# Turning the second batch's first half by DMA instead of on TensorE, in a fused attention and SwiGLU kernel

## The chip, the cores and the metric

One core of a Trainium2 chip. The metric is the device time of the whole kernel in microseconds (us), median of several runs. "Slot" below is a place in the kernel's own schedule, not a time: two slots per step of the feed-forward part. PE is TensorE, ACT ScalarE, DVE VectorE, POOL GpSimd, SP SyncE. A transfer lands when all its completions are counted. A packet is one DMA record of the trace: 1024 or 512 bytes of a load, 256 of a transpose.

## The reference, cut to what matters

```python
def _attn_ref(q, k, v, E, F):                 # q, k, v: (8, 8, 1024, 64), E, F: (64, 1024)
    k_proj = einsum('ks,bhsd->bhkd', E, k)
    v_proj = einsum('ks,bhsd->bhkd', F, v)
    scores = q @ k_proj^T / sqrt(64)
    attn   = softmax(scores)                  # 64 columns
    return attn @ v_proj
x   = attn_out as (8192, 512)                 # tokens x (heads * 64)
g   = x @ w_gate;  val = x @ w_val            # 512 x 1536
out = (g * sigmoid(g) * val) @ w_out          # 1536 x 512
```

## The kernel before

Each of the 8 batches is cut into two halves of 512 tokens. While PE does the feed-forward part of one half, the attention units of a later one are strewn between its matmuls. Two turns are needed in each half: q (so that heads' channels lie on the partitions) and the softmaxed attention (so that its 64 columns do). They are done on PE or by a DMA transpose:

```python
BY_DMA = [(b, ch) for b in range(1, B) for ch in range(CH)][1:]   # all but batch 0 and half (1, 0)

def u_T(b, u):                # q turn on PE: four transposes, one copy
    for n in range(4):
        nc.tensor.transpose(out=ps[:, n, :], in_=..., identity=ident_bf[:])
    copy(eng, t[:], ps[:])

def u_TD(b, ch):              # q turn of a half by DMA, on SP's queue
    nc.sync.dma_start_transpose(out=t[:], in_=qb[b, ch][:]...)

def u_AD(b, ch):              # attention turn of a half by DMA, on SP's queue
    nc.sync.dma_start_transpose(out=t[:]..., in_=AA.pop((b, ch, "d"))[:]...)

def u_S(b, u): ...            # scores on PE, exp on ACT
def u_R(b, u): ...            # sum and reciprocal on DVE
def u_N(b, u): ...            # normalise on POOL, into AA (PE turn) or AAd (DMA turn)
def u_PV(b, ch, pr): ...      # PE: attention times v, reads AT
```

The loads `load_q`, `load_k`, `load_v` and those of weights are issued by POOL and cast from f32 to bf16 on the way, so the place of a load among POOL's `u_N` units decides when it starts. [...] The q, k and v pools hold enough buffers for the next batch.

The softmax here doesn't subtract the row's maximum and nothing guards it: scores larger than these inputs give would overflow.

## Time and profile before

| | before |
|---|---|
| median | 573.17 us (572.98 to 573.52, 4 runs) |
| PE busy | 564.2 of 571.7 us |
| PE's waits after 33 us | none over 0.2 us |
| DMA engines, 0 to 86 us | full |
| DMA transposes | 26, landing 4.3 to 17.5 us after issue |

How to read it: PE sets the time, so only PE work or a wait of PE counts. The first 86 us, in which the DMA engines are full, are where a transfer can come too late. The lines are in the prediction.

### The profile page before, as it was taken

The numbers are of one execution on the slowest core, as the hardware profiler recorded it, in microseconds if no ns is written. First come the engines' busy times: TensorE is split into PE (matmuls) and PEld (weight loads), VectorE is DVE, ScalarE is ACT, GpSimd is POOL, SyncE is SP. The second block draws the span as 40 slices with busy tenths as digits, with TensorE's granted clock in tenths as the row PEclk, the third lists the DMA queues.
The fourth block names the chain that finished last, engine by engine and source line by source line (L and its number), as shares of the span: only waits on it lengthen the run. The fifth ranks groups of instructions, "written<-read, shape, count | busy, mean of one in ns | idle before, by whom it ended". The sixth has DMA issues, their size and how long they took to land.

```text
span 571.7 us, 7944 instructions
## 1 busy us (share of the span) xinstructions
PE 564.2 (99%) x2971; PEld 268.5 (47%) x2971; DVE 336.6 (59%) x581; ACT 238.3 (42%) x421; POOL 109.2 (19%) x122
## 2 busy tenths in 40 slices
PE   8999999999999999999999999999999999999997
PEld 4644444444444444444444444444444444444444
DVE  3677566666466654666556665567546674554540
ACT  3555434354435434444335434354342543443232
POOL 6834121134002500124001330023200220000000
PEclk9999999999999999999999999999999999999999
DMA  9999993549901697038940499204990124100012
GB/s 202 176 199 206 202 177 77 89 71 197 202 29 47 113 192 148 19 75 129 196 100 37 64 176 196 63 20 90 196 176 37 44 50 75 38 37 23 33 38 92
DMA packets 106983, 61.86 MB, mean 108 GB/s; under 512 B 60096, under 2 KB 98240, under 8 KB 106944
## 3 DMA queue, kind: packets, MB, share of 16 engines
q0 software_dynamic: 42800, 29.36, 35.7%
q1 hardware_dynamic: 63232, 30.42, 24.7%
q10 hardware_dynamic: 912, 1.57, 1.0%
q8 instruction: 23, 0.38, 0.3%
q14 instruction: 16, 0.13, 0.1%
HBM read 60.29 MB, written 16.78 MB: 135 GB/s over the span
## 4 chain that ended last, share of the span: by engine, by line
PE 92%; DMA 3%; DVE 2%; POOL 1%; ACT 1%; issue 0%; DVEq 0%; POOLq 0%
PE yps L362 29%; PE vps L324 27%; PE gps L324 27%; PE kvp L149 3%; PE sc L229 2%; PE pv L287 2%; DMA wv<-in_moe_w_val_dram 2%; DMA qb<-in_q_dram 1%; DVE zz L244 1%; POOL AA L260 0%; POOL wg L117 0%; PE qTp L195 0%; DVE hT L348 0%; ACT xT L137 0%; DVE s L343 0%
## 5 line engine op out<-in xcount | busy, mean ns | idle before, releaser
L343 DVE SCALAR_TENSOR_TENSOR s<-th,gps 128x512 f32<-128x512 f32 x192 | 130.5, 680 | 139.2 <-ACT th L336 138.8
L324 PE MATMUL gps<-xT,wg 128*128 128x512 bf16 (+1 forms) x776 | 197.8, 377 | 0.7 <-DMA wg<-in_moe_w_gate_dram 0.4
L324 PE MATMUL vps<-xT,wv 128*128 128x512 bf16 (+1 forms) x776 | 197.5, 377 | 0.1
L362 PE MATMUL yps<-wo,hT 128*128 128x512 bf16 (+1 forms) x780 | 194.5, 376 | 0.0
L336 ACT ACTIVATE th<-gps 128x512 f32<-128x512 f32 x192 | 114.6, 597 | 163.4 <-PE gps L324 161.9
L348 DVE TENSOR_TENSOR hT<-s,vps 128x512 bf16<-128x512 f32 x192 | 132.0, 687 | 22.1 <-PE vps L324 1.5
L362 PEld LDWEIGHTS <-hT 128*128 128x128 bf16 x780 | 76.2, 98 | 89.9
L260 POOL TENSOR_TENSOR AAd<-ee,rr 128x512 bf16<-128x512 f32 x52 | 54.1, 1040 | 319.5 <-issue 178.1
L324 PEld LDWEIGHTS <-wv 128*128 128x128 bf16 x776 | 73.8, 98 | 83.2 <-issue 3.3
L324 PEld LDWEIGHTS <-wg 128*128 128x128 bf16 x776 | 74.0, 98 | 81.9 <-DMA wg<-in_moe_w_gate_dram 0.9
L372 ACT ACTIVATE ysb<-yps 128x512 f32<-128x512 f32 (+1 forms) x65 | 38.4, 590 | 78.1 <-PE yps L362 78.1
L137 ACT CAST xT<-pv 128x512 bf16<-128x512 f32 x63 | 36.7, 584 | 51.2 <-PE pv L287 50.3
L244 DVE TENSOR_REDUCE zz<-ee 128x8 f32<-128x512 f32 x64 | 43.5, 679 | 19.4 <-ACT ee L233 19.4
L233 ACT ACTIVATE ee<-sc 128x512 f32<-128x512 f32 x64 | 37.9, 596 | 18.0 <-PE sc L229 17.9
L287 PE MATMUL pv<-AT,BDV 128*128 128x512 bf16 x60 | 22.6, 379 | 0.0
L229 PEld LDWEIGHTS <-qTd 128*128 128x128 bf16 x208 | 16.0, 98 | 12.3
L229 PE MATMUL sc<-BD,qTd 128*128 128x128 bf16 x208 | 20.1, 219 | 0.0
L137 DVE CAST BDV<-kvp 64x256 bf16<-64x256 f32 x14 | 6.0, 427 | 22.1 <-ACT ks L159 19.1
L260 POOL TENSOR_TENSOR AA<-ee,rr 128x512 bf16<-128x512 f32 x11 | 11.4, 1038 | 36.3 <-DVE rr L246 34.4
L246 DVE RECIPROCAL rr<-zz 128x8 f32<-128x8 f32 x64 | 13.0, 203 | 6.7 <-DVE zz L244 0.5
L149 PE MATMUL kvp<-vb,FT 128*64 128x512 bf16 (+2 forms) x80 | 15.7, 339 | 0.3 <-ACT BDV L137 0.3
L149 PE MATMUL kvp<-kb,ET 128*64 128x512 bf16 (+1 forms) x72 | 15.5, 358 | 0.3 <-DVE kb L137 0.2
(51 smaller groups left out, 146.4 us busy)
## 6 DMA issues: line engine op xcount, KB each, us to landing
out_dram<-ysb SPq DMA_DIRECT2D x63, 256.0 KB, 2.4
qb<-in_q_dram POOLq DMA_DIRECT2D x15, 512.0 KB, 16.9
kb<-in_k_dram POOLq DMA_DIRECT2D x7, 1024.0 KB, 11.3
vb<-in_v_dram POOLq DMA_DIRECT2D x7, 1024.0 KB, 14.0
wo<-in_moe_w_out_dram POOLq DMA_DIRECT2D x2, 768.0 KB, 15.3
wg<-in_moe_w_gate_dram POOLq DMA_DIRECT2D x5, 256.0 KB, 9.6
wv<-in_moe_w_val_dram POOLq DMA_DIRECT2D x5, 256.0 KB, 10.2
kraw<-in_k_dram ACTq DMA_DIRECT2D x2, 512.0 KB, 5.0
```

The costliest lines, as they stand in the source:

```text
L137: (nc.scalar.copy if eng is nc.scalar else eng.tensor_copy)(out=out, in_=in_)
L149: nc.tensor.matmul(out=t[lo : lo + 64, h0:h1].rearrange("p h d -> p (h d)"), lhsT=w[:, j, :], rhs=src[b][:, h0:h1, j, :], start=(j == 0), ...
L229: nc.tensor.matmul(out=ps[:, n, :], lhsT=t[:, n, :], rhs=BD[b % 2][:, 4 * g + n, :], start=True, stop=True)
L233: nc.scalar.activation(out=e[:].rearrange("p h j k -> p (h j k)"), in_=ps[:].rearrange("p a k -> p (a k)"), func=AF.Exp, scale=scale,)
L244: nc.vector.reduce_sum(out=z[:], in_=e[:], axis=AX.X)
L260: eng.tensor_tensor(out=a.rearrange("p j h k -> p h j k"), in0=ee.pop((b, u))[:], in1=rr.pop((b, u))[:].unsqueeze(3).to_broadcast([P, 4, 2 ...
L324: nc.tensor.matmul(out=ps[:, ts], lhsT=(wg, wv)[w][:, kt, f * P : (f + 1) * P], rhs=x[:, kt, ts], start=(kt == 0), stop=(kt == NKT - 1),)
L336: nc.scalar.activation(out=th[:], in_=ps[:], func=AF.Tanh, scale=0.5)
L343: nc.vector.scalar_tensor_tensor(out=s1[:], in0=th[:], scalar=1.0, in1=g[:], op0=ALU.add, op1=ALU.mult)
L348: nc.vector.tensor_tensor(out=hT[c][:, f, :], in0=s1[:], in1=ps[:], op=ALU.mult)
L362: nc.tensor.matmul(out=yy[c][:, cs], lhsT=hT[c][:, f, i * P : (i + 1) * P], rhs=wo[:, f, cs], start=(f == 0), stop=(f == NFT - 1),)
L372: nc.scalar.activation(out=ysb[:, cs], in_=yy[c][:, cs], func=AF.Copy, scale=0.5)
```

## The change

Its intent: take the last 32 turns of the second batch off PE. To make room for the two added DMA transposes, the first q half and k of the second batch are loaded ahead of the output weights, the projections and scores are moved, and the third batch's loads, whose k and v were issued at 47.6 and 48.5 us until now, wait on POOL behind the fourth normalised unit, that is until the input of the attention transpose is ready.

```diff
-BY_DMA = [(b, ch) for b in range(1, B) for ch in range(CH)][1:]
+BY_DMA = [(b, ch) for b in range(1, B) for ch in range(CH)]
 ...
         if b == 1:
+            put(22, u_TD, 1, 0)
+            put(29, u_KV, 1, "k")
+            put(32, u_KT, 1)
+            put(40, u_KV, 1, "v")
+            sa = (35, 36, 37, 38, 43, 44, 45, 47)
+            put(41, u_AD, 1, 0)
             put(30, u_TD, 1, 1)
-            put(34, u_KV, 1, "k")
-            put(36, u_KT, 1)
-            put(40, u_KV, 1, "v")
-            sa = (37, 38, 39, 40, 48, 50, 52, 54)
-            tt = (35, 36, 37, 38)
-            ta = (41, 42, 43, 44)
-            put(57, u_AD, 1, 1)
-            sp = (43, 44, 45, 46, 66, 67, 68, 69)
+            put(50, u_AD, 1, 1)
+            sp = (44, 45, 46, 46, 66, 67, 68, 69)
         else:
-            put(s0, u_KV, b)
+            put(s0 + (6 if b == 2 else 0), u_KV, b)
 ...                                       # the third batch's other units move a few slots too
+        load_q(1, 0)
+        load_k(1)
         load_wo(0)
         load_wo(1)
-        load_k(1)
 ...
-            s0 = 48 * (b - 1) - (12 if b == 2 else 24)
-            put(s0, load_k, b)             # and v, q, q two slots apart
+            s0 = 48 * (b - 1) - (20 if b == 3 else 24)
+            at = (40, 40, 41, 42) if b == 2 else (s0, s0 + 2, s0 + 4, s0 + 6)
+            put(at[0], load_k, b)          # and v, q, q at at[1], at[2], at[3]
```

More of the change, by code (lines that the diff above doesn't have):

```diff
@@ L394, in place @@
         if b == 1:
-            put(30, u_TD, 1, 1)
-            put(34, u_KV, 1, "k")
-            put(36, u_KT, 1)
-            put(40, u_KV, 1, "v")
-            sa = (37, 38, 39, 40, 48, 50, 52, 54)
-            tt = (35, 36, 37, 38)
-            ta = (41, 42, 43, 44)
-            put(57, u_AD, 1, 1)
-            sp = (43, 44, 45, 46, 66, 67, 68, 69)
-        else:
-            put(s0, u_KV, b)
-            put(s0 + 3, u_KT, b)
-            o = 14 if b == 2 else 6
-            put(s0 + (3 if b == 2 else -6), u_TD, b, 0)
-            put(s0 + (5 if b == 2 else -4), u_TD, b, 1)
+            put(22, u_TD, 1, 0)
[4 more added lines that the diff above has]
+            put(41, u_AD, 1, 0)
+            put(30, u_TD, 1, 1)
+            put(50, u_AD, 1, 1)
+            sp = (44, 45, 46, 46, 66, 67, 68, 69)
+        else:
+            put(s0 + (6 if b == 2 else 0), u_KV, b)
+            put(s0 + (9 if b == 2 else 3), u_KT, b)
+            o = 13 if b == 2 else 6
+            put(s0 + (7 if b == 2 else -6), u_TD, b, 0)
+            put(s0 + (9 if b == 2 else -4), u_TD, b, 1)
             sa = [s0 + o + 3 * j for j in range(NJ)]
@@ L414, in place @@
         for j in range(NJ):
-            if (b, j // 4) not in BY_DMA:
-                put(tt[j], u_T, b, j)
-                put(ta[j], u_A, b, j)
             put(sa[j], u_S, b, j)
@@ L549 @@
         put(23, u_PV, 0, 1, 3)
-        put(20, load_q, 1, 0)
         put(20, load_v, 1)
@@ L555 @@
         for b in range(2, B):
-            s0 = 48 * (b - 1) - (12 if b == 2 else 24)
-            put(s0, load_k, b)
-            put(s0 + 2, load_v, b)
-            put(s0 + 4, load_q, b, 0)
-            put(s0 + 6, load_q, b, 1)
+            s0 = 48 * (b - 1) - (20 if b == 3 else 24)
+            at = (40, 40, 41, 42) if b == 2 else (s0, s0 + 2, s0 + 4, s0 + 6)
+            put(at[0], load_k, b)
+            put(at[1], load_v, b)
+            put(at[2], load_q, b, 0)
+            put(at[3], load_q, b, 1)
         for s in slots:
```

## The prediction

> **What bounds the kernel now.** I read the page's busy shares and slices first, then PE's own waits, then PE's instructions in order of time, then the DMA transposes. The page:
>
> ```profile
> PE 564.2 (99%) x2971; PEld 268.5 (47%) x2971; DVE 336.6 (59%) x581; ACT 238.3 (42%) x421; POOL 109.2 (19%) x122
> ...
> PE   8999999999999999999999999999999999999997
> ...
> DMA  9999993549901697038940499204990124100012
> ```
>
> Each digit is one fortieth of 571.7 us, 14.3 us. PE is full in every slice but the ends; no other engine passes 59%. The DMA engines are full in the first six slices, 0 to 86 us, which is where all of the second batch's preparation lies. So the change can gain only PE time, and can lose only where a late transfer makes PE wait.
>
> PE's waits, in us, times, longest:
>
> ```profile
> PE efp L455 <- DMA Eraw<-in_E_dram: 0.8, 1, 0.8
> PE gps L324 <- DMA wg<-in_moe_w_gate_dram: 0.4, 1, 0.4
> PE kvp L149 <- ACT BDV L137: 0.3, 1, 0.3
> ```
>
> These and the other six all fall before 33 us. In the windows from 58 us to 560 us PE is busy for the whole of every window: no idle time can absorb or hide anything there.
>
> PE in order of time (start, duration, line) around the turns that the change removes:
>
> ```profile
> 62.47 0.39 PE L195 MATMUL qTp<-ident_bf,qb 128*128 128x128 bf16 x4
> 62.69 1.03 PE L324 MATMUL gps<-xT,wg 128*128 128x512 bf16 x4
> ...
> 75.17 0.39 PE L276 MATMUL aTp<-ident_bf,AA 128*128 128x128 bf16 x4
> 75.39 1.03 PE L324 MATMUL gps<-xT,wg 128*128 128x512 bf16 x4
> ```
>
> What counts is start to next start: four turns hold PE 62.47 to 62.69, 0.22 us, 55 ns each, though their records say 0.39 us together and 219 ns each. The ends are modelled and overlap.
>
> The transposes by DMA, as they are already done for the other 13 half batches (issue time in ns min/median/max; then us from issue to landing):
>
> ```profile
> L207 SPq DMA_TRANSPOSE qTd<-qb x13: 1782/3082/7293, 63.0 to 423.2; - x13
> ...
> DMA to landing us min/median/max: 4.3/4.9/13.0
> ```
> ```profile
> L214 SPq DMA_TRANSPOSE AT<-AAd x13: 1316/3715/8099, 102.6 to 472.1; - x13
> ...
> DMA to landing us min/median/max: 4.3/5.7/17.5
> ```
>
> The spread is the point: 4.3 us on idle DMA engines (the one issued at 102.6), 13.0 (issued at 63.0) and 17.5 (issued at 125.7) when loads run beside it.
>
> **What the Trainium skill says.** "TensorE: Matmul & The Clock Gate", Back-to-back issue gap, gives N/2.4 + 2.5 ns for one warm matmul, 56 ns at 128 columns and 216 at 512, but 81 and 131 for a sustained stream. This trace agrees with the first pair (55 ns a turn; four 512-column matmuls every 0.86 us, 216 each) and not with the second. Part 4 of that page, PE-mode transpose, has about 275 ns in one kernel's context; here a record is 219 ns and the spacing 55, and the spacing is the cost. "DMA: Bandwidth & Descriptors", Queues, rings and completion order, says that a DMA engine serves its queue rows in turn, packet by packet. The packet records agree: between 67.5 and 72.5 us each half microsecond has 74 to 77 load packets of 1024 bytes and 74 to 78 transpose packets of 256 bytes, where the transpose alone gets about 425 and the load alone about 102. A transpose has 2048 data packets, so beside such loads it needs about 13.4 us, alone 2.4.
>
> **The change, part by part.** Only the first half of the second batch still turned on PE.
>
> Removed from PE: four q turns and four attention turns of four instructions, 32 x 55 ns = 1.76 us. The eight spacings read directly (0.22, 0.24, 0.22, 0.22 and 0.22, 0.23, 0.22, 0.22) sum to 1.79. All of it is in saturated PE time, so all of it is on the path that sets the end. The built order confirms it: 64 PE rows less (32 loads of weights, 32 matmuls), and nothing added on PE.
>
> Removed beside PE: four ACT copies of 0.58 us and four DVE copies of 0.4 us. Worth nothing, neither bounds.
>
> Added: two DMA transposes on SP's queue and their wait for data. PE pays only if one is late. I place them from landings in the trace of before: the last value weights land at 38.6 to 40.1 us; a q half takes 2.65 us of full DMA, a k or v 5.05, half of wo 3.8.
>
> (a) First q half and k are now issued ahead of wo. Estimates: q lands at 42.5, k at 47.6. The k projection now stands at about 52.7 us on PE (two and a half f steps earlier than its 58.0): 5 us to spare.
>
> (b) The q transpose goes out at 42.5. The one at 63.0 showed its first packet 3.5 us after issue; then 13.4 us beside loads of wo and v: it lands at about 60. Its first user, the scores, stands at about 62.7 on PE. To spare: 2 to 3 us. wo then lands at 52.6 and 57.7, needed at 58.4 and 61.0: enough.
>
> (c) The second q half lands at about 66 instead of 63.0. Its transpose then meets idle engines, since the third batch's loads are held back, and lands near 70.8. PE uses it at about 77.
>
> (d) The attention transpose is the tight one. The fourth scores stand at 66.8 on PE; exp, the sum behind a 0.69 us hT on DVE, and 1.04 us on POOL end at about 70.9. SP issues then, and POOL lets k and v of the third batch go at the same moment. The first product with v stands at about 78.8: 7.9 us. Alone it takes 4.3; beside full loads from the first packet it would take 14. But a load that starts on idle engines starts slowly: after the one issued at 121.6 there were 33 packets in the microsecond from 123.0 to 124.0, and at full rate about 204. So the transpose should have most of its packets through before the loads fill: estimate 5.5 to 7.5 us, so landing between 76.4 and 78.4.
>
> (e) The third batch's k and v, issued at 47.6 and 48.5 before, now go at about 71; v lands near 87 to 89. The change moves its projection six slots later, to about 94.
>
> Later batches keep their work; their loads shift by four slots at most. Sum with no new wait: 573.08 - 1.76 = 571.3 us.
>
> **The rivals.**
>
> 1. A late attention transpose takes the place of the removed work. For it: round robin with 1024-byte packets, the 13.0 and 17.5 us seen, and a release of loads at the very same instant. Against it: the slow start of those loads, and the extra slots between the fourth unit and the first product. If the loads win from the first packet, it lands at about 85 and PE waits 6 us: 577.5, slower by 0.8%. A mild case is 1 to 2 us of wait: 572.5 to 573.5, no gain at all.
>
> 2. A late q transpose, case (b). For it: it runs wholly beside loads, and 17.5 us was seen. Against it: the 17.5 had an output queued ahead of it, this one has nothing. At 17.5 it would land at 60.0, still before 62.7. Its cost, if any, is 1 to 2 us.
>
> 3. The third batch's v or q too late for the moved projection, since the loads start 22 us later. For it: they carry about 15 us of DMA work, and two transposes and outputs share it. Against: the slack of 5 us or more. Beyond it PE would stall at about 94 us.
>
> 4. DMA becomes the bound everywhere. Against it: after 86 us the slices hold zeros and fours, and the bytes added are two transposes beside 26.
>
> **Range and chances.** No gain above about 1.8 us exists to be had, so the low end is 571.3 less the noise of some 0.3 and a little for a neighbouring gap: 570.8. I give 0.3 to a wait in rival 1, mean 2 us, and about 0.1 each to 2 and 3, of 1 to 2 us; high end 574.3. The middle: 571.5. Two per cent is 11.5 us. Nothing can win that, and only several late transfers together could lose it.
>
> **What would show it.** Right: 64 rows less on PE; busy PE down from 564.2 to about 562.4; no PE wait after 33 us; the attention transpose of this half in 5 to 8 us. The step that fails is visible by name: a PE wait of pv on AT is rival 1, of sc on qTd rival 2, of kvp on vb or kb at about 94 us rival 3. My placing of the loads is wrong if the q transpose lands after 61 us or the third batch's v after 92. The prediction is wrong beyond its range if PE idles over 3 us between 50 and 130 us, or if time goes that I have no part for.

## More of the kernel before

The granted clock is the share of its full clock that the profile shows TensorE to have had.

## The result, and the profile after

579.80 us median (579.32 to 580.27, 4 runs) against 573.17: slower by 6.6 us. The ratio is 1.0115, 95% interval 1.0097 to 1.0132. A ratio here is the mean time of one kernel's fast runs over that of the other's of the same rounds, so it is not quite the ratio of the medians quoted.

The page of the changed kernel, busy shares and slices:

```profile
PE 561.2 (97%) x2883; PEld 267.3 (46%) x2939; DVE 335.2 (58%) x577; ACT 236.7 (41%) x417; POOL 109.1 (19%) x122
...
PE   8999959999999999999999999999999999999997
...
PEclk9999989999999999999999999999999999999999
DMA  9999899508950499027970299413991023010002
```

PEld has 32 instructions less (2971 to 2939), as the built order said. Some matmul records are missing, so the loads of weights are the better count. New is the 5 in PE's sixth slice, 72 to 87 us, and the 8 in the clock beside it: PE stood still there, once. The list of PE's waits names it:

```profile
PE pv L287 <- DMA AT<-AAd: 5.9, 1, 5.9
```

And PE in order of time (start, duration, line, and in brackets the idle time before):

```profile
78.22 0.39 PE L229 MATMUL sc<-BD,qTd 128*128 128x128 bf16 x4
84.50 0.61 PE L287 MATMUL pv<-AT,BDV 128*128 128x512 bf16 x1 [5.89 <-DMA AT<-AAd]
84.90 1.91 PE L324 MATMUL vps<-xT,wv 128*128 128x512 bf16 x4
86.60 0.63 PE L362 MATMUL yps<-wo,hT 128*128 128x512 bf16 x1
```

The first product with v needs the attention transpose. By start times, the four scores hold PE until 78.44; then nothing until 84.50. After it, four 512-column matmuls take from 84.90 to 86.60, 1.70 us instead of 0.86: PE runs at half speed. The windows say so (us, then PE, PEld, DVE, ACT, POOL busy with counts, granted clock, DMA share, GB/s):

```profile
82.00:84.00 2.00, 0.00 (x0) 0.00 (x0) 0.00 (x0) 0.00 (x0) 0.00 (x0) 0.64 1.19 244
84.00:86.00 2.00, 1.50 (x4) 0.59 (x5) 0.00 (x0) 0.58 (x1) 0.00 (x0) 0.50 1.24 217
86.00:88.00 2.00, 1.78 (x5) 0.72 (x5) 1.15 (x2) 0.00 (x0) 0.00 (x0) 0.50 1.26 205
88.00:90.00 2.00, 2.00 (x11) 1.03 (x10) 0.67 (x3) 0.96 (x2) 1.04 (x1) 0.65 1.35 202
90.00:92.00 2.00, 2.00 (x11) 0.91 (x10) 1.48 (x4) 1.68 (x4) 1.04 (x1) 1.00 1.41 199
```

The last column but two is the granted clock. "TensorE: Matmul & The Clock Gate", Part 1, says that PE's clock falls to one half after an idle window of about 3.4 us and comes back after about as long under load. This trace agrees in kind: half from 82.57, 4.1 us into the standstill, to 89.39, 4.9 us after PE went on. The length does not settle it: e10 below lost the clock 2.7 us into its standstill, e4 with a standstill of 2.7 us in all, and e1 kept it through 3.15.

The sum of it: between the first product at 84.50 and the second pair of them at 90.15 stand three groups of 0.86 and three of 0.22 us at full speed, 3.24 us; it took 5.65, so the clock cost 2.4. With 6.06 us of standstill (78.44 to 84.50) and 1.79 us less work that is +6.7, beside +6.6 measured.

What the transpose met (SP's queue, then POOL, in order of time; then the transpose's landing):

```profile
71.08 2.68 SPq L214 DMA_TRANSPOSE AT<-AAd  x1
```
```profile
70.01 1.04 POOL L260 TENSOR_TENSOR AAd<-ee,rr 128x512 bf16<-128x512 f32 x1 [1.06 <-ACT ysb L372]
71.00 0.94 POOL L88 DMA_DIRECT2D kb<-in_k_dram  x1
71.94 0.88 POOL L98 DMA_DIRECT2D vb<-in_v_dram  x1
72.80 1.77 POOL L107 DMA_DIRECT2D qb<-in_q_dram  x2
```
```profile
DMA to landing us min/median/max: 13.4/13.4/13.4
```

The fourth normalised unit ends, and the same 0.1 us starts the transpose and the first of four loads. Packets in the trace by half microsecond:

```
from us   load packets   transpose packets (of 2048)
72.0        0               74
72.5        0              192
73.0        0              332
73.5        5              340
74.0       32              236      so far 1174
74.5       22               37
75.0       13               34
76.0       40               58
78.0       55               63
80.0       66               65
81.0       64               70
```

Once the loads arrive the transpose goes from 340 packets per half microsecond to 34, and the last 874 packets take 8.1 us, to 82.56. Its completions then come late too: twelve of sixteen by 82.99, the last at 84.45.

### The profile page after: what moved, and what is told of

It is laid out like the page before. It is cut to its first block, busy times and chain, and to the rows that moved or that the text cites. A ratio compares the mean times of both kernels' runs of the same rounds, so it can differ in the third digit from the quotient of the medians.

```text
span 578.1 us, 7823 instructions
## 1 busy us (share of the span) xinstructions
PE 561.2 (97%) x2883; PEld 267.3 (46%) x2939; DVE 335.2 (58%) x577; ACT 236.7 (41%) x417; POOL 109.1 (19%) x122
## 4 chain that ended last, share of the span: by engine, by line
PE 89%; DMA 5%; DVE 2%; POOL 1%; issue 1%; ACT 1%; ACTq 0%; DVEq 0%; POOLq 0%
PE yps L362 28%; PE vps L324 27%; PE gps L324 26%; PE kvp L149 2%; DMA AT<-AAd 2%; PE sc L229 2%; PE pv L287 2%; DMA wv<-in_moe_w_val_dram 2%; DMA kraw<-in_k_dram 1%; DVE zz L244 1%; POOL AA L260 0%; POOL wg L117 0%; DVE hT L348 0%; PE qTp L195 0%; ACT xT L137 0%
## 5 line engine op out<-in xcount | busy, mean ns | idle before, releaser
L324 PE MATMUL gps<-xT,wg 128*128 128x512 bf16 (+1 forms) x755 | 195.5, 377 | 1.8 <-DMA wg<-in_moe_w_gate_dram 0.6
L362 PE MATMUL yps<-wo,hT 128*128 128x512 bf16 (+2 forms) x759 | 192.2, 377 | 1.0 <-issue 0.2
L260 POOL TENSOR_TENSOR AAd<-ee,rr 128x512 bf16<-128x512 f32 x56 | 58.2, 1040 | 351.8 <-issue 157.2
L229 PEld LDWEIGHTS <-qTd 128*128 128x128 bf16 x224 | 17.4, 99 | 13.5 <-issue 0.5
L229 PE MATMUL sc<-BD,qTd 128*128 128x128 bf16 x224 | 21.9, 221 | 0.1
L107 POOL DMA_DIRECT2D qb<-in_q_dram x17 | 15.5, 914 | 0.6 <-DMA wv<-in_moe_w_val_dram 0.6
```

What stands on the lines that cost most here:

```text
L229: nc.tensor.matmul(out=ps[:, n, :], lhsT=t[:, n, :], rhs=BD[b % 2][:, 4 * g + n, :], start=True, stop=True)
L260: eng.tensor_tensor(out=a.rearrange("p j h k -> p h j k"), in0=ee.pop((b, u))[:], in1=rr.pop((b, u))[:].unsqueeze(3).to_broadcast([P, 4, 2 ...
L324: nc.tensor.matmul(out=ps[:, ts], lhsT=(wg, wv)[w][:, kt, f * P : (f + 1) * P], rhs=x[:, kt, ts], start=(kt == 0), stop=(kt == NKT - 1),)
L362: nc.tensor.matmul(out=yy[c][:, cs], lhsT=hT[c][:, f, i * P : (i + 1) * P], rhs=wo[:, f, cs], start=(f == 0), stop=(f == NFT - 1),)
```

## The experiments

**Theory A**: the four loads, released at the same instant, slow the attention transpose by taking turns with it, and PE waits for it. **Rival B**: it is late for another reason, its own queue or its place in the program. **Rival C**: part of the loss is not the wait but the clock after it. A fourth, that the moved loads and projections cost time by themselves, is tested in the second group. Comparisons are with the kernel before of the same rounds on the same chip: 572.77 us in the first group, 573.04 in the second, 573.14 in the third.

### e1_late: loads five slots later

```diff
-at = (40, 40, 41, 42) if b == 2 else ...
+at = (45, 45, 46, 47) if b == 2 else ...
```

> The changed kernel, but the third batch's four loads stand behind the fifth normalised unit of the second batch instead of the fourth, some 8 us later. Theory A (the loads released at the same instant slow the attention transpose packet by packet): the transpose lands 4.3 to 5 us after issue instead of 13.4, at about 76 us, PE's wait of pv on AT of 5.9 us and the half clock after it are gone; v of the third batch is now late for the moved projection, a wait of kvp of 0 to 3 us; time 571.3 to 574.5. Rival B (the transpose is late for another reason: its own queue, SP, or the place in the program): it still lands after 80 us and the time stays at 577 or more.

575.36 us (574.86 to 577.05, 4 runs), ratio 1.0047. The loads now start at 80.95 instead of 71.00. The transpose took 4.3 us, and the wait of pv on AT is gone. In its place stands the prediction's third rival:

```profile
PE kvp L149 <- DMA vb<-in_v_dram: 3.0, 1, 3.0
```

The time came out just above the expected span. B falls: nothing was changed but the loads' start. Starting them later than needed has its own price. PE stood for 3.15 us here and the clock of the profiled run stayed at 1.00 up to 125 us.

### e2_gate: loads let go by the landed transpose

```diff
+    gate = const.tile([P, 1], BF16, name="gate")
+    def u_gate(b, ch):
+        nc.gpsimd.tensor_copy(out=gate[:], in_=AT[b, ch][:, 0, 0, 0:1])
 ...
+            put(42, u_gate, 1, 0)
-at = (40, 40, 41, 42) if b == 2 else ...
+at = (43, 43, 43, 43) if b == 2 else ...
```

> The changed kernel, but GpSimd first reads one element of the landed attention transpose and only then lets the third batch's loads go, so that they start right behind it. Theory A: the transpose lands at about 75.5 to 76 us, the loads go at about 76, v lands at about 90 before its projection at 94; no wait of PE on any of them; time 571.0 to 572.0, below both kernels. Rival B: the transpose still takes over 10 us, the loads go at 83 or later, and the time is 580 or more.

571.86 us (571.37 to 572.06, 4 runs), ratio 0.9980 (0.9965 to 0.9995). As expected, no wait of PE after 33 us.

### e3_warm: PE kept at work in the standstill

```diff
+    def u_warm(n):                 # n matmuls of zeros, 128x512, read by nobody
+            put(44, u_warm, 28)
```

> The changed kernel with 28 idle matmuls of 512 columns (6.05 us at full clock) ahead of the second scores of the half, where PE otherwise stands still. Theory C (after the standstill the granted clock is one half for some 5.6 us, which costs 2.4 us on top of the wait): the transpose lands as late as before, the granted clock stays at 1.0 and the time falls by 2.4 to about 577.4. Rival: the clock costs nothing of its own (the slow stretch is waits for other engines): time stays at 579.5 to 580.

578.09 us (577.07 to 579.27, 4 runs), ratio 1.0084: 1.7 us below the changed kernel, but that was on another chip, so it is taken up again below.

### e4_qfirst: the loads with small packets first

```diff
-at = (40, 40, 41, 42) if b == 2 else ...      # k, v, q, q
+at = (42, 42, 40, 40) if b == 2 else ...      # q, q, k, v
```

> The changed kernel, but of the third batch's loads the two q halves (512-byte packets) go first and k and v (1024-byte packets) behind them; the release is at the same instant, and the same bytes follow. Theory A with turns packet by packet: a transpose packet waits for half as long a load packet, the transpose takes about 8 to 10 us instead of 13.4, lands at 79 to 81; PE's wait is 0.5 to 2.5 us; time 572.5 to 576. Rival (DMA time is shared by bytes, or the slow start of any load is what counts): it lands no earlier than 82, time 578 to 580.

575.64 us (574.69 to 576.08, 4 runs), ratio 1.0045. The transpose:

```profile
DMA to landing us min/median/max: 10.0/10.0/10.0
```

It landed at 81.2, a little after the expected 79 to 81, and PE waited 2.5 us for it. The same bytes at the same instant, in packets of 512 instead of 1024 bytes at first, cost 3.4 us less. From 75.0 to 77.5 the trace has 89 to 114 load packets and 96 to 111 transpose packets per half microsecond: turns go by number of packets, not by bytes. The turns between queues that "DMA: Bandwidth & Descriptors", Queues, rings and completion order, describes agree with these counts. A packet of that page is a group of several descriptors, so whether the turn changes at each record of the trace is not shown.

The clock was lost here too, though PE stood for only 2.7 us (78.56 to 81.25):

```profile
82.00:84.00 2.00, 2.00 (x6) 0.76 (x5) 0.89 (x2) 0.26 (x1) 0.00 (x0) 0.50 1.20 253
```

It was half from 81.79 to 85.20, and from the first product to the second pair took 4.94 us instead of 3.24: 1.7 us lost. In e1 a longer standstill lost nothing in the profiled run. (The three runs of e1 at a clock of 1.000 took 574.86 to 575.56 us, the one at 0.997 took 577.05, so it may have been lost there.) Over these traces the half-clock stretches last 3.41, 6.83, 6.83 and 17.07 us (e4, the changed kernel, e10, e7), whole multiples of 3.41 us, and begin 2.7 to 4.1 us after PE stopped, in e4 even 0.5 us after it went on. A wait shorter than the page's idle window can thus cost the clock.

### e5_qonly: only the q turns by DMA

```diff
 def u_N:  if (b, ch) in BY_DMA:   ->   if (b, ch) in BY_DMA[1:]:
-            put(41, u_AD, 1, 0)
+            ta = (41, 42, 43, 44)         # u_A(1, 0..3) on PE again
```

> One part alone: the changed kernel with only the q turns of the half by DMA; its four attention turns stay on PE (16 instructions of 55 ns) and there is no attention transpose for it. Loads and slots as changed. Theory A: no new wait at all, PE work 0.88 us below the kernel before: 572.1 to 572.8 where before is 573.0. A rival that blames the q transpose or the moved projection finds a wait of sc on qTd or of kvp on vb of some us, and 575 or more.

571.86 us (571.33 to 571.96, 4 runs), ratio 0.9977 (0.9962 to 0.9992), a little below the expected span. No new wait: the q transpose is innocent, though it too ran beside loads (61.3 - 42.1 = 19.2 us from issue to landing). Half of the change is faster than before.

### e6_moves: the moves alone, both turns on PE

```diff
-BY_DMA = [...]
+BY_DMA = [...][1:]
-            put(22, u_TD, 1, 0)
-            put(41, u_AD, 1, 0)
+            tt = (33, 34, 35, 36);  ta = (41, 42, 43, 44)
```

> The moves alone: loads, projections and slots as in the changed kernel, but both turns of the half on PE as before, so no transpose by DMA is added. Theory A (only the attention transpose meeting the loads costs time): no wait, the same PE work as before, time within 0.5 us of the kernel before. Rival (the later loads and the moved projection cost time by themselves): slower by over 1 us, with a wait of kvp on kb or vb near 94 us.

573.11 us (572.72 to 575.91, 4 runs), ratio 1.0011 (0.9986 to 1.0036). The moves are neutral by the median. One of the four runs was 3 us longer at a granted clock of 0.997; only the first was profiled, so what PE waited for in that one stays open.

### e7_early: the loads not held back

```diff
-at = (40, 40, 41, 42) if b == 2 else ...
+at = (36, 38, 40, 42) if b == 2 else ...
```

> Undo the holding back of the third batch's loads: they stand at the slots of the kernel before (k right behind the second q half, v and q behind later units), all else as changed. Theory A: now the second q transpose too meets loads (13 us, lands at about 78 to 82, a wait of sc on qTd of 1 to 4 us) and the attention transpose stands behind it on the same queue and beside v: it lands at 84 to 90; time 580 to 588, worse than the changed kernel. Rival (holding the loads back is what costs): faster than the changed kernel, under 578.

586.50 us (583.72 to 588.59, 4 runs), ratio 1.0219 (1.0177 to 1.0261). PE's waits:

```profile
PE pv L287 <- DMA AT<-AAd: 9.4, 1, 9.4
PE sc L229 <- DMA qTd<-qb: 3.8, 1, 3.8
```

The attention transpose landed 20.5 us after issue, at 93.5, later than the 84 to 90 expected. So holding the loads back is right; they were held back a little too short.

### e8_delay1: one microsecond more

```diff
+    def u_pad():                   # 128x512, 1.04 us on POOL, read by nobody
+        nc.gpsimd.tensor_tensor(out=pad[:], in0=zeros[:], in1=zeros[:], op=ALU.mult)
+            put(40, u_pad)
-at = (40, 40, 41, 42) if b == 2 else ...
+at = (41, 41, 41, 42) if b == 2 else ...
```

> The changed kernel with one idle GpSimd instruction of about 1 us between the fourth normalised unit and the third batch's loads. In the changed kernel the transpose had 1174 of its 2048 packets through when the loads' packets came, and 874 more need about 1.0 us alone. Theory A with an all-or-nothing edge: 1 us more alone lets it land at 75.5 to 77.5 us, no wait of PE, time 571.4 to 572.6: one us of delay is worth some 8 us. Rival (the slowing is in proportion to how long both run together, or the issue of the loads on GpSimd slows it): lands at 80 or later, time 577 or more.

571.09 us median of 570.73, 571.03, 571.16 and 575.93; ratio 0.9985 (0.9944 to 1.0026). In the profiled run the transpose moved 404 to 434 packets in each half microsecond from 72.0 to 74.0; all its data was through at 74.46, before the first load packet at 74.88. Its completions came only from 76.6 to 77.7, when the loads had started; in the gated kernel the landing follows 0.5 us after the last data packet. That the loads held the completions up is likely, not shown. It landed 7.0 us after issue, and the first product did not wait. An edge, as expected: one microsecond of delay is worth over 8 us in three runs of four. The run of 575.93 (clock 0.996) is not profiled; e12 bears on it.

### e9_gate5, e10_after5, e11_warm5, e12_delay2

The gated kernel again, the changed kernel and the warm one side by side, and two idle units instead of one (`put(40, u_pad)` twice).

> The kernel whose loads wait for the landed attention transpose, again with more rounds, to settle whether it is below the kernel before. With all of the removed 1.76 us kept: 1.2 to 2.0 us below before (ratio 0.9965 to 0.998), no run above the kernel before. If it only seemed faster: ratio 0.999 or more.

571.07 us (570.71 to 571.61, 5 runs), ratio 0.9962 (0.9949 to 0.9974): below both kernels, settled. POOL of this run in order of time:

```profile
74.67 0.19 POOL L215 COPY gate<-AT 128x1 bf16<-128x1 bf16 x1 [4.33 <-DMA AT<-AAd]
74.91 0.94 POOL L88 DMA_DIRECT2D kb<-in_k_dram  x1
```

and PE where the changed kernel stood still:

```profile
77.51 0.39 PE L234 MATMUL sc<-BD,qTd 128*128 128x128 bf16 x4
77.74 0.38 PE L292 MATMUL pv<-AT,BDV 128*128 128x512 bf16 x1
```

The transpose is issued at 70.37 and landed after 4.2 us; the product follows the scores without a gap.

> The changed kernel itself on the same chip, so that the next run has its own comparison: 579 to 580.5, a wait of pv on AT of 5 to 7 us, granted clock about 0.994.

579.51 us (579.19 to 579.96, 4 runs), ratio 1.0110; wait 5.9 us, transpose 13.4 us from issue to landing. The result repeats.

> The kernel with idle matmuls in PE's standstill, again, beside the changed kernel of the same call. The clock costs 2.4 us of its own by the trace: the mean should be 1.7 to 2.8 us below the changed kernel, with a granted clock of 1.0. If the clock costs nothing: within 0.5 us of it.

579.15 us (578.85 to 579.73, 4 runs): only 0.36 us below e10. The expectation missed. The clock is as expected, here in the warm kernel:

```profile
84.00:86.00 2.00, 0.94 (x9) 0.46 (x7) 0.00 (x0) 0.60 (x1) 0.00 (x0) 1.00 1.18 246
86.00:88.00 2.00, 2.00 (x11) 0.94 (x12) 0.77 (x2) 0.58 (x1) 0.00 (x0) 1.00 1.23 215
```

From the first product to the second pair it took 3.26 us (85.94 to 89.20), in e10 4.98 (84.62 to 89.60): the clock's part there is 1.7 us, and it fell 2.7 us into the standstill. But the transpose now landed later:

```profile
DMA to landing us min/median/max: 14.6/14.6/14.6
```

14.6 us, and 14.1 in e3, against 13.4 in both runs of the changed kernel. The idle matmuls won back the clock and lost most of it again to a later landing. Why is not shown. The traces have one candidate: in both runs with idle matmuls a 16,384-byte instruction fetch begins while the transpose is under way (82.44 and 81.92 us), and some 0.8 us later load and output packets take up to 1.36 us each, where without the idle matmuls none took over 0.73 from 76 to 87 us; in both runs of the changed kernel that fetch begins at 88.05 and 88.16, after the landing.

> Two idle GpSimd instructions (2.1 us) between the fourth unit and the third batch's loads; one gave 571.0 three times and 575.9 once, so the edge lies near 1 us. With two, the loads' first packets come at about 76, after the transpose has landed: no run above 573, median within 0.5 us of the gated kernel. If a run near 576 comes again, its cause is not the edge of this transpose.

571.51 us (571.19 to 571.78, 5 runs), ratio 0.9970 (0.9957 to 0.9984); the transpose landed after 4.9 us. No run near 576, so the one in e8 may be the edge of one microsecond. But e6 had a run as long (575.91) with no attention transpose at that place, at a clock of 0.997 beside 0.996 in e8: what those two runs waited for stays open.

## Why the prediction was wrong

**The removed work: right.** The trace from the first to the last weight load of the output projection takes 510.02 us in e6 and 508.23 in the gated kernel, which have the same units and no wait in between: 1.79 us, the sum of the eight spacings. The changed kernel takes 516.69 there: 8.46 us more, the 6.06 of standstill and 2.40 of the clock. From the 193rd of those loads to the last, all kernels take 375.72 us: nothing after 200 us changed.

**Parts (a), (b), (c): no wait, as predicted, with less to spare.** k landed at 47.2 (47.6 predicted), the first q transpose at 61.1 (60) before its use at 62.2, the second at 70.0 (70.8). The q transpose took 19.3 us, longer than the 17.5 feared, and left 1.1 us instead of 2 to 3; by the prediction's own sign (61 us) the loads were placed slightly wrong. e5 shows that no wait hangs on these.

**Part (e): too early.** v landed at 92.8, not 87 to 89, past the sign of 92. In e5, where no attention transpose ran beside it, the same load landed at 86.6.

**Part (d), the landing of the attention transpose: the step that failed.** It read: "the transpose should have most of its packets through before the loads fill: estimate 5.5 to 7.5 us, so landing between 76.4 and 78.4". It landed at 84.45, 13.4 us after issue. The runs show three things in place of that estimate.

- Crowding. I took few load packets to mean much time left over. But in the starting phase the packets themselves are slow: 125 to 290 ns a load packet on average by half microsecond from 74.0 to 77.0, 98 at full rate, and 171 and 212 ns a transpose packet from 74.5 to 75.5, 24 before. The transpose ran at 34 to 70 per half microsecond, below the 74 to 78 beside a load at full rate. So the 874 packets left at 74.5 took 8.1 us.
- A slow start of the transpose itself, before any load packet. In the microsecond from its first packet it moved 430, the gated one 788; in all five profiled runs in which SP and POOL issue within 0.1 us of each other it was 404 to 453, in the five in which it starts alone or 0.9 us ahead 781 to 797. SP's issuing record was 2.7 us instead of 1.9. POOL's issuing alone does not do it: in e8 POOL issued k and v from 71.56 on, and the transpose moved 786. Why it starts slowly stays open.
- The completions: 1.9 us from the last data packet to the landing, 0.5 in the gated run.

It took both of the first two, by an estimate from these numbers. At the gated run's pace 1816 packets instead of 1174 would have been through by 74.5; the other 232 would have needed some 2 us beside the loads, and with 1.9 us for the completions the landing comes to about 78.3, inside the predicted span. Without the crowding the 874 would have needed about 1 us. No run separates the two: e8 removed both at once.

**Rival 1: the right mechanism, given too little weight and one term too few.** Its hard case said 85 us, a wait of 6 us and 577.5; it was 84.45, a wait of 5.9 and 579.8. The missing term is the clock: 2.4 us in this trace, 1.7 in e10. "TensorE: Matmul & The Clock Gate", Part 1, names the effect, and I did not price it: a wait of PE of 2.5 us or more may have to be priced with the restart (1.7 us in e4 after 2.5, nothing in e1's profiled run after 3.0).

**Rival 2: refuted by e5. Rival 3: absent in the changed kernel**, whose standstill moved the projection to 102 us, but v landed at 92.8 instead of 87 to 89, and with the standstill away and the loads 10 us later it came true in e1, with 3.0 us. **Rival 4: refuted**, as the equal last 375.72 us show; its reading of the DMA slices was wrong, which hold nines too after 86 us.

**A slip of no weight.** Batch 0 is turned on PE as well, before and after.

**The range.** 570.8 to 574.3 held the gated version, not the change. Its upper end took rival 1 at its mild size with a chance of 0.3. The honest reading of an 8 us margin against a transfer that takes 4.3 or 13 us, depending on a race of two issues 0.1 us apart, would have been two outcomes, not one with a tail.

## What to carry to other kernels

Here a DMA transpose of many small packets took 4.2 to 4.9 us when loads were held back until it was through, and 13.4 when they were released with it. Do not release bulk loads at the event that starts a transpose that is needed soon; release them at its landing, by letting the issuing engine touch one element of the result, and not much later (e1). Price a late transfer twice: the wait, and the clock of TensorE after it, which cost 1.7 to 2.4 us in three of the traces and nothing in e1's.

## What the Trainium skill lacked or had wrong

- "DMA: Bandwidth & Descriptors", Queues, rings and completion order: nothing is said of a load's first microseconds, in which the packets of both queues are slow: 34 to 70 transpose packets per half microsecond beside a starting load, 74 to 78 beside a running one, some 420 alone.
- No page has it: a transpose issued by SP within 0.1 us of a load issued by POOL moved 404 to 453 packets in its first microsecond, and 781 to 797 otherwise, with no load packet yet (two in e4).
- "TensorE: Matmul & The Clock Gate", Back-to-back issue gap: its 131 ns for a sustained stream of 512 columns is not seen here; four take 0.86 us, 216 ns each, at full clock in every trace of this case.
- No page has it: with 28 idle matmuls in PE's standstill the same transpose beside the same loads landed after 14.1 and 14.6 us, without them after 13.4 twice. The cause is not shown.
